# Which early load carries the first k, and which k the weights' loads wait for, in a fused linear-attention and GELU-MLP kernel

## The chip, the cores and the metric

The kernel runs on one core of a Trainium2 chip. The metric is the device time of one execution in microseconds (us). Before the change three runs gave 172.68, 172.98 and 173.50 us, so a median of 172.98. The profile was taken in an execution of its own, which took 173.12 us; its trace spans 171.3 us, and 1.8 us lie around the span.

## What is computed

A recurrent attention with a decay per key feature runs over 768 tokens in each of 4 batches and 8 heads of 48 features; its output, 3072 tokens of 384 features, goes through an MLP of width 2048 with the tanh form of GELU.

```
def _attn_ref(q, k, v, alpha):
    for t in range(S):
        state = alpha[:, :, t, :, None] * state + np.einsum('bhd,bhe->bhde', k[:, :, t], v[:, :, t])
        y[:, :, t] = np.einsum('bhd,bhde->bhe', q[:, :, t], state)

x = attn_out.transpose(0, 2, 1, 3).reshape(B * S, H * D)
h = x @ w_in
g = 0.5 * h * (1.0 + np.tanh(c * (h + 0.044715 * h * h * h)))
out = g @ w_out
```

## The kernel before

**Tiling.** The 768 tokens are cut into 6 chunks of 128. A *unit* is one chunk of two batches; there are 12 units, 0 to 11, and unit 0 and unit 1 are the two halves of chunk 0. In each unit the recurrence is done as matrix products: the logarithm of alpha (`ln`, on ScalarE, called ACT) is summed along the tokens by a product with a triangle of ones (`cum`, on TensorE, called PE), `b` and `binv` are its exponentials with either sign (ACT), `qp` and `kp` are q and k scaled by them (VectorE, called DVE), `t` turns them on PE and `ev` copies the turned tile out (ACT or DVE), `attn` is the product of turned k and q (PE), `mask` keeps its triangle (DVE), `vb` casts v (ACT or DVE), `y` is the attention output (PE), `x` copies it out, `tx` turns it and `xe` copies that. `kv` and `st` carry the state to the next chunk; `bend`, `end` and, from unit 3 on, `rows` (four 32-wide transposes on DVE, L466) prepare the decay of the state. Then `l1` (L684) is the first MLP product in 8 pieces of 6 matmuls for a unit, `gelu` follows on ACT, `l2` (L703) is the second product in 4 pieces of 4 matmuls for each batch of the unit, and `ot` and `store` bring the result out. A name such as `l10.6` is piece 6 of `l1` for unit 0, `kp0.1` the second `kp` of unit 0. In units 0 and 1 the two batches go through `ln`, `cum`, `qp`, `kp`, `t` and `attn` one by one.

**Buffers that order the work.** PSUM is given out by a planner: `ff` has 4 banks (for `l1`, `l2`, the `cum` of units 0 and 1, idle products and some `attn`), `yk` has 2 (for `t`, `y`, `tx`, `kv`), `ca` holds one tile. A task that takes a bank waits until its former users are done.

**Order.** `Scheduler.order` (L64) lists every task. Up to about 45 us the order is the list `FIRST` (L189), written out by hand: `P:` is PE, `V:` DVE, `A:` ACT, `G:` GpSimd (called POOL), `S:` SyncE (called SP). `fill.n` stands for n idle products of 512 columns (L318), which keep PE busy. Behind the list the planner picks by rank; `SHIFT` (L236) changes ranks, and `AFTER` (L242) adds a dependency. `W` and `LANDED` hold the planner's costs and landing times; they move only the planned order, and nothing in the program waits for them.

**Early loads.** `RINGS` (L185) lists the loads that SP or ACT issue, `load.0` to `load.11`: both alphas of unit 0 (`load.0`, `load.1`), then q and k of its first batch (`load.2`, `load.3`), q and k of its second batch (`load.4`, `load.5`), and the same six of unit 1. `BY_ACT = (2, 3,)` (L187) gives `load.2` and `load.3` to ACT. `LOADS` (L182) lists what POOL issues: v of unit 0 (`load.12`), `w_in` in four parts (`load.13`, `15`, `16`, `17`), v of unit 1 (`load.14`, between the first and second part), `w_out` in four parts, and the inputs of the later units. An entry `gatek 0 1` is a copy of one element of k on POOL (L343), which waits until that load has landed; everything that POOL issues behind it waits with it. So `gatea 0 1` holds the load of v until the second alpha of unit 0 is there, and `gatek 0 1` holds `w_in` until the k of the second batch of unit 0 is there. The program calls the two batches of a unit 0 and 1, which is what the last digit means.

The loads are L334 (SP and ACT), L337 (POOL, rows) and L359 (POOL, `w_in`).

Of the kernel before, what the change touches and what calls it, by code (L numbers as in the profile page):

```python
# [16 lines left out]
    cum=530, cum_packed=1500, t8=450, t4=225, attn=340, kv=170, inter=165, intra=203, tx=168, l1_4=655, l1_2=340, l2=651,  # L17
    qk2=880, qk1=500, ev8=610, ev4=350, mask=610, st=1065, st0=545, end=110, attn2=600, vb=320, vb_act=480, ring=1300, ring_issue=670, out=2050, lead=600, receipt=1400, receipt_hw=1000, xc=475, xe=275, ot=540,
    ev8_act=920, ev4_act=520, xc_act=385, xe_act=400, ot_act=450,
    strip=1700, cast=1450, weight=2080, dma=2100, issue=1100, wissue=760, sp=420, store=2600, turn=1250, landed=2200, xbar_qk=1500, xbar_x=1400, turn_lead=50, stored=300, turn_receipt=200, rows=1400, ones=205, late_qk=1700, late_x=1700, late_x6=500, piece=330, late_k=1500, piece_issue=450, begin=620, cast_0=1300, share=1200, cast_1=1900, ln_packed=1040, cold=380, t64=640, fill=216, zero=1100,  # L20
)
COST = {
    ("ACT", "b"): (385, 135), ("ACT", "binv"): (385, 135), ("ACT", "ev"): (600, 40), ("ACT", "gelu"): (510, 110),
# [151 lines left out]
class _Kernel:  # L175
# [3 lines left out]

    SPLIT = (2,)  # L180
    EARLY = (0, 1)
    LOADS = ('gatea 0 1', 'v0', 'gatek 0 1', 'in 0', 'v1', 'in 1', 'in 2', 'in 3', 'out 0', 'out 1', '2a', 'out 2', '2b', 'out 3', '3', '4', '5', '6', 'a7', 'q7', 'hold k 5', 'k7', 'v7', 'a8', 'hold k 6', 'q8', 'k8', 'a9', 'hold k 7', 'v8', 'q9', 'k9', 'hold k 8', 'v9', 'a10', 'q10', 'hold x 7', 'k10', 'a11', 'hold k 9', 'q11', 'k11', 'v10', 'hold k 10', 'v11')  # L182

    PACKED, CUM_FF, R = (0, 1), (0, 1), 4
    RINGS = (('a', 0, 0, 1), ('a', 0, 1, 2), ('q', 0, 0, 1), ('k', 0, 0, 1), ('q', 0, 1, 2), ('k', 0, 1, 2),  # L185
             ('a', 1, 0, 1), ('a', 1, 1, 2), ('q', 1, 0, 1), ('k', 1, 0, 1), ('q', 1, 1, 2), ('k', 1, 1, 2))
    BY_ACT = (2, 3,)  # L187

    FIRST = """  # L189
        A:table.0 A:load.2 A:load.3 S:load.0 S:load.1 S:load.4 A:ln0.0 S:load.5 P:fill.7 P:cum0.0 A:ln0.1 G:gate.0 G:load.12 S:load.6 P:cum0.1 A:b0.0 S:load.7  # L190
        A:bend0.0 V:qp0.0 A:binv0.0 A:binv0.1 S:load.8 V:kp0.0 P:fill.2 P:t0.0 A:b0.1 V:ev0.0 P:fill.1 P:t0.1 S:load.9 A:ev0.1 V:qp0.1 S:load.10 A:bend0.1
        P:fill.3 P:attn0.0 V:kp0.1 G:gate.1 S:load.11 P:t0.2 G:load.13 V:mask0.0 A:ev0.2 P:t0.3 G:load.14 V:mask0.1 A:ev0.3 P:fill.1 P:t0.4 V:ev0.4 P:fill.1
        P:attn0.1 A:ln1.0 G:load.15 P:t0.5 V:mask0.3 P:cum1.0 A:ev0.5 G:load.16 V:vb0.0 A:ln1.1 V:end0.0 P:y0.0 V:mask0.2 G:load.17 P:kv0.0 A:binv1.0 P:cum1.1
        V:st0.0 A:x0.0 G:load.18 A:vb0.1 V:kp1.0 P:tx0.0 A:b1.0 P:y0.1 V:xe0.0 G:load.19 V:qp1.0 P:t1.1 A:x0.1 A:bend1.0 G:load.20 A:b1.1 P:fill.1 P:t1.0
        A:ev1.0 V:ev1.1 G:load.21 V:qp1.1 P:fill.1 P:kv0.1 V:st0.1 G:load.22 A:binv1.1 P:tx0.1 P:attn1.0 V:xe0.1 G:load.23 P:t1.2 V:kp1.1 P:l10.0 A:ev1.2
        G:load.24 V:mask1.0 P:t1.3 A:bend1.1 P:t1.4 V:mask1.1 G:load.25 A:ev1.3 P:l10.1 V:ev1.4 G:load.26 A:vb1.0 P:t1.5 P:attn1.1 G:load.27 V:ev1.5 P:y1.0
        G:load.28 P:l10.3 V:end1.0 V:vb1.1 V:mask1.2 G:load.29 A:gelu0.0 P:kv1.0 P:l10.2 V:mask1.3 A:x1.0 G:load.30 P:l10.5 A:gelu0.1 V:st1.0 A:gelu0.3 P:y1.1
        G:load.31 P:l10.4 A:gelu0.5 V:x1.1 P:tx1.0 A:gelu0.2 P:tx1.1 P:l10.6 G:load.32 V:xe1.1 A:gelu0.4 V:xe1.0 P:l10.7 A:gelu0.6 G:load.33 P:l11.0 A:gelu0.7
        P:l11.6 A:gelu1.0 P:l11.5 A:gelu1.6 P:l11.7 A:gelu1.5 P:l11.2 A:gelu1.7 P:l11.4 A:gelu1.2 P:l11.3 A:gelu1.4 P:l11.1 A:gelu1.3 P:kv1.1 P:l20.0
        A:gelu1.1 P:l20.4 P:l20.1 A:ln2.0 P:l20.2 P:cum2.0 P:l20.5 A:b2.0 A:binv2.0 P:l20.9 A:bend2.0 V:kp2.0 A:ln2.1 P:l20.6 V:st1.1 P:cum2.1 V:qp2.0 P:l20.8  # L200
        A:b2.1 A:binv2.1 P:t2.0 P:l20.3 V:kp2.1 A:ev2.0 V:qp2.1 P:l20.10 A:bend2.1 P:attn2.0 P:t2.1 V:mask2.1 P:l20.7 A:ev2.1 V:mask2.0 P:l20.14 A:ln3.0
        P:attn2.1 P:y2.0 V:mask2.2 P:l20.13 V:mask2.3 P:l20.12 V:x2.0 P:cum3.0 A:ot0.0 V:ot0.1 P:y2.1 A:ot0.2 S:store0.0 S:store0.1 P:tx2.0 P:l20.11 A:x2.1
        S:store0.2 V:xe2.0 A:b3.0 P:tx2.1 P:l20.15 V:xe2.1 A:binv3.0 V:end2.0 P:l12.0 V:ot0.3 P:l12.1 V:qp3.0 S:store0.3 P:kv2.0 P:l12.2 V:st2.0
        A:gelu2.0 P:l12.3 V:kp3.0 A:gelu2.1 P:l12.4 A:gelu2.2 P:t3.0 A:gelu2.3 V:ev3.0 A:gelu2.4 P:l12.5
    """.split()
    LANDED = {"load.0": 2800, "load.1": 3400, "load.2": 4400, "load.3": 5000, "load.4": 6000, "load.5": 7300, "load.12": 10100, "load.6": 9200, "load.7":
              10000, "load.8": 10500, "load.9": 11000, "load.10": 11600, "load.11": 12000, "load.13": 14100, "load.14": 16000, "load.15":
              17800, "load.16": 19200, "load.17": 21100, "load.18": 23500, "load.19": 24800, "load.20": 26400, "load.21": 27100, "load.22":
              27900, "load.23": 28300, "load.24": 30100, "load.25": 31000, "load.26": 31900, "load.27": 32600, "load.28": 32900, "load.29":
              34800, "load.30": 36700, "load.31": 38400, "load.32": 41200, "load.33": 42600}  # L210

    NARROW = (0, 1)

# [20 lines left out]
    PIECES = (0, 192, 320, 384)  # L234

    SHIFT = {  # L236
        'b10.0': 557, 'b6.0': 10, 'b9.0': -173, 'binv8.0': -756, 'kp9.0': -733, 'kv3.1': -567, 'mask3.1': 47, 'mask7.2': -293, 'mask7.3': -104,
        'mask8.0': 10, 'mask8.1': 43, 'qp6.0': -300, 'qp7.0': 100, 'rows7.0': 100, 'st3.0': 127, 'tx3.1': -30, 'tx4.0': -60, 'tx5.0': 1204,
        'x7.1': -400,
    }  # L240

    AFTER = {  # L242
        'cum6.0': 'y4.0',
    }

    ROW_ENDS = (3, 4, 5, 6, 7, 8, 9)
# [484 lines left out]
    def tasks(self):  # L731
        s = self.s = Scheduler(self.BUFS, self.fill, 40000, self.FIRST, self.LANDED)
        B, NCH = self.B, self.NCH
# [341 lines left out]
```

## Time and profile before

| what | value |
|---|---|
| median of three runs | 172.98 us |
| the profiled execution | 173.12 us |
| its span | 171.3 us |
| PE busy | 165.6 us (97%) |
| ACT busy | 128.8 us (75%) |
| DVE busy | 102.8 us (60%) |
| POOL busy | 58.8 us (34%) |
| DMA, mean | 175 GB/s |

Busy time is the time in which an engine executes. A PE that executes idle products counts as busy. The chain of waits is followed back from the last instruction: at each step it goes to what released the instruction, so it names the work on which the end hangs. The timeline shows the instructions of an engine in order, with the idle time in front of them and what ended it. "To landing" of a load is the time from its issue until its last part is in SBUF. All times below count from the start of the span.

### The profile page before, as it was taken

Reading aid. Unit: us, or ns where it says so; the run is one execution under the profiler, and the core shown is the slowest. Engines: PE = TensorE matmul, PEld = TensorE weight load, DVE = VectorE, ACT = ScalarE, POOL = GpSimd, SP = SyncE. Lnnn points to the kernel's source line nnn. Section 1 sums busy time; section 2 is a strip of 40 time slices with the busy share of each in tenths; the row PEclk is TensorE's granted clock in tenths of the full one; section 3 lists DMA queues with packets and bytes.
Section 4 is the critical chain, followed back from the end, with each engine's and each line's share of the span. In section 5 each row is a group of like instructions: output and inputs, shape, how many; then the busy total and the mean of one; then the engine's idle time right before and its main releaser. Section 6 shows DMA issues by size and latency. Waiting matters only on the chain.

```text
span 171.3 us, 4477 instructions
## 1 busy us (share of the span) xinstructions
PE 165.6 (97%) x1851; PEld 130.3 (76%) x1853; DVE 102.8 (60%) x210; ACT 128.8 (75%) x214; POOL 58.8 (34%) x71
## 2 busy tenths in 40 slices
PE   7889999999999999999999999999999999999993
PEld 2556999666886896796697697797796796886973
DVE  6399940166889999797896798695640825100000
ACT  3568899846979897788798599399798992572831
POOL 2397446997655400096008009402503000000000
PEclk9999999999999999999999999999999999999999
DMA  4999999999999999789998999996799961401102
GB/s 129 308 255 230 204 245 232 226 228 203 214 305 200 236 253 167 97 182 243 216 221 102 211 167 142 236 255 141 208 139 150 126 157 31 138 0 50 46 0 92
DMA packets 53652, 29.91 MB, mean 175 GB/s; under 512 B 41728, under 2 KB 50048, under 8 KB 53632
## 3 DMA queue, kind: packets, MB, share of 16 engines
q0 software_dynamic: 26464, 17.70, 63.0%
q1 hardware_dynamic: 26624, 11.54, 33.8%
q10 hardware_dynamic: 544, 0.39, 0.8%
q8 instruction: 14, 0.23, 0.6%
q14 instruction: 6, 0.05, 0.1%
HBM read 25.17 MB, written 4.72 MB: 174 GB/s over the span
## 4 chain that ended last, share of the span: by engine, by line
PE 91%; DMA 3%; ACT 3%; DVE 1%; issue 0%; DVEq 0%
PE hT L684 37%; PE acc L703 37%; PE at L583 4%; DMA k<-in_k_dram 3%; PE yps L649 2%; PE cum L416 2%; PE kv L600 2%; PE qkT_ps L488 2%; PE yps L563 1%; PE xT_ps L672 1%; PE yps L641 1%; ACT qkT L506 1%; PE k_ps L534 1%; ACT L309 1%; PE qkT_ps L519 1%; PE idle L318 1%
## 5 line engine op out<-in xcount | busy, mean ns | idle before, releaser
L703 PE MATMUL acc<-w_out,gT 128*128 128x384 bf16 (+3 forms) x416 | 68.5, 314 | 0.0
L684 PE MATMUL hT<-xT,w_in 128*128 128x256 bf16 x576 | 67.9, 273 | 0.0
L684 PEld LDWEIGHTS <-w_in 128*128 128x128 bf16 x576 | 61.5, 114 | 1.4
L690 ACT ACTIVATE gT<-hT 128x512 bf16<-128x512 f32 x96 | 54.1, 604 | 5.7 <-PE hT L684 2.6
L703 PEld LDWEIGHTS <-gT 128*128 128x128 bf16 x416 | 37.2, 98 | 20.2
L590 DVE TENSOR_TENSOR atm<-at,ut 128x512 bf16<-128x512 f32 x48 | 30.2, 683 | 6.6 <-PE at L583 6.4
L715 ACT COPY ot<-acc 128x384 f32<-128x384 f32 (+3 forms) x21 | 9.3, 446 | 17.0 <-PE acc L703 16.3
L478 DVE TENSOR_TENSOR kp<-k,binv 128x768 bf16<-128x768 f32 (+1 forms) x15 | 11.9, 795 | 15.6 <-ACT binv L450 14.9
L351 POOL CAST gate<-qkT 128x1 f32<-128x1 bf16 x6 | 1.1, 189 | 50.2 <-DMA qkT<-kp 50.2
L478 DVE TENSOR_TENSOR qp<-q,b 128x768 bf16<-128x768 f32 (+1 forms) x15 | 11.9, 792 | 8.1 <-ACT b L450 8.1
L450 ACT ACTIVATE b<-cum 128x768 f32<-128x768 f32 (+1 forms) x15 | 10.3, 684 | 5.3 <-PE cum L416 3.4
L337 POOL DMA_DIRECT2D k<-in_k_dram x11 | 12.2, 1110 | 5.6 <-DMA vb<-in_v_dram 2.5
L337 POOL DMA_DIRECT2D a<-in_alpha_dram x11 | 12.3, 1117 | 3.5 <-DMA w_in<-in_moe_w_in_dram 1.3
L337 POOL DMA_DIRECT2D vb<-in_v_dram x11 | 12.2, 1109 | 3.7 <-PE hT L684 0.9
L337 POOL DMA_DIRECT2D q<-in_q_dram x11 | 12.2, 1113 | 3.5 <-DMA w_out<-in_moe_w_out_dram 1.0
L466 DVE STREAM_TRANSPOSE rows<-b 32x256 f32<-32x256 f32 x28 | 12.3, 439 | 0.5
L309 ACT ACT_TABLE_LOAD x9 | 11.5, 1283 | 0.9 <-PEq L1059 0.7
L450 ACT ACTIVATE binv<-cum 128x768 bf16<-128x768 f32 (+1 forms) x15 | 10.2, 683 | 2.2 <-PE cum L416 2.1
L690 ACT ACT_TABLE_LOAD x9 | 11.5, 1283 | 0.2
L623 DVE TENSOR_TENSOR stmp<-kv,st 128x384 f32<-128x384 f32 x16 | 8.8, 553 | 1.2 <-PE kv L600 1.1
L626 DVE TENSOR_TENSOR st<-stmp,ends 128x384 bf16<-128x384 f32 x16 | 8.9, 558 | 0.6
L399 ACT ACTIVATE la<-a 128x768 f16<-128x768 f32 (+1 forms) x11 | 8.7, 787 | 0.1
(83 smaller groups left out, 142.7 us busy)
## 6 DMA issues: line engine op xcount, KB each, us to landing
out_dram<-ot SPq DMA_DIRECT2D x19, 192.0 KB, 4.6
a<-in_alpha_dram POOLq DMA_DIRECT2D x9, 384.0 KB, 9.6
q<-in_q_dram POOLq DMA_DIRECT2D x9, 384.0 KB, 8.6
k<-in_k_dram POOLq DMA_DIRECT2D x9, 384.0 KB, 9.2
vb<-in_v_dram POOLq DMA_DIRECT2D x9, 192.0 KB, 9.5
w_in<-in_moe_w_in_dram POOLq DMA_DIRECT2D x4, 384.0 KB, 8.9
w_out<-in_moe_w_out_dram POOLq DMA_DIRECT2D x4, 384.0 KB, 11.1
out_dram<-ot SPq DMA_DIRECT2D x9, 96.0 KB, 5.0
```

Of the source, the lines that this page charges most:

```text
L309: nc.scalar.add_instruction(mybir.InstLoadActFuncSet(name=nc.get_next_instruction_name(), act_func_set_id=i, engine=mybir.EngineType.Activ ...
L337: dma(u[t][:, lo:hi].rearrange("t b h d -> t (b h) d"), src.rearrange("b h s d -> s (b h) d")[c * C:(c + 1) * C])
L450: self.nc.scalar.activation(u[n].rearrange("t i h d -> t i (h d)")[:, lo:hi], cum, AF.Exp, scale=1.0 if n == "b" else -1.0)
L466: nc.vector.transpose(t[f:f + 32], bass.AP(last.tensor, last.offset + o * D + 32 * half, [list(last.ap[0]), [2 * D, H], [1, 32]]))
L478: self.nc.vector.tensor_tensor(out, rows, b, op=ALU.mult)
L590: self.nc.vector.tensor_tensor(u["atm", i][:, o], u["at", i][o], self.ut[:, None, :].to_broadcast([self.C, self.H // 2, self.C]), op=ALU.mult)
L623: nc.vector.tensor_tensor(s, acc, old, op=ALU.add)
L626: nc.vector.tensor_tensor(new.rearrange("f p (o d) -> f (p o) d", o=2), acc.rearrange("f p (o d) -> f (p o) d", o=2), ends, op=ALU.mult)
L684: self.nc.tensor.matmul(h[:, s], w_in[:, j, nt % 4 + s], self.xT[c % self.NX][:, lo:hi, j], start=j == 0, stop=j == self.NKT - 1, skip_gro ...
L690: return lambda e: self.nc.scalar.activation(self.gT[c % self.NG][:, nt:nt + 2, lo * self.C:hi * self.C], f.pop(("h", c, lo, nt)), AF.Gelu ...
L703: self.nc.tensor.matmul(f["acc", c, b][:, lo:hi], self.gT[c % self.NG][:, nt, b * self.C:(b + 1) * self.C], self.w_out[:, nt, lo:hi], star ...
L715: self.copy(e)(f["ot", c, b][:, sl], f["acc", c, b] if half is None else f["acc", c, b, half][:, sl])
```

## The change

Three things are edited, and the order is made anew around them.

1. `BY_ACT` loses `load.3`: the k of the first batch of unit 0 is issued by SP, third in its queue, behind both alphas. ACT issues only `load.2`.
2. `gatek 0 1` becomes `gatek 0 0`: POOL's loads of the weights wait for that first k.
3. `FIRST`, `LANDED`, `W["rows"]`, `SHIFT` and `AFTER` are new. The same products stand in another order.

The core of the diff, with the whole list of early steps up to the first pieces of `l1`:

```diff
-    LOADS = ('gatea 0 1', 'v0', 'gatek 0 1', 'in 0', 'v1', 'in 1', 'in 2', 'in 3', 'out 0', 'out 1', '2a', 'out 2', '2b', 'out 3', '3', '4', '5', '6', 'a7', 'q7', 'hold k 5', 'k7', 'v7', 'a8', 'hold k 6', 'q8', 'k8', 'a9', 'hold k 7', 'v8', 'q9', 'k9', 'hold k 8', 'v9', 'a10', 'q10', 'hold x 7', 'k10', 'a11', 'hold k 9', 'q11', 'k11', 'v10', 'hold k 10', 'v11')
+    LOADS = ('gatea 0 1', 'v0', 'gatek 0 0', 'in 0', 'v1', 'in 1', 'in 2', 'in 3', 'out 0', 'out 1', '2a', 'out 2', '2b', 'out 3', '3', '4', '5', '6', 'a7', 'q7', 'hold k 5', 'k7', 'v7', 'a8', 'hold k 6', 'q8', 'k8', 'a9', 'hold k 7', 'v8', 'q9', 'k9', 'hold k 8', 'v9', 'a10', 'q10', 'hold x 7', 'k10', 'a11', 'hold k 9', 'q11', 'k11', 'v10', 'hold k 10', 'v11')
...
-    BY_ACT = (2, 3,)
+    BY_ACT = (2,)
...
-        A:table.0 A:load.2 A:load.3 S:load.0 S:load.1 S:load.4 A:ln0.0 S:load.5 P:fill.7 P:cum0.0 A:ln0.1 G:gate.0 G:load.12 S:load.6 P:cum0.1 A:b0.0 S:load.7
-        A:bend0.0 V:qp0.0 A:binv0.0 A:binv0.1 S:load.8 V:kp0.0 P:fill.2 P:t0.0 A:b0.1 V:ev0.0 P:fill.1 P:t0.1 S:load.9 A:ev0.1 V:qp0.1 S:load.10 A:bend0.1
-        P:fill.3 P:attn0.0 V:kp0.1 G:gate.1 S:load.11 P:t0.2 G:load.13 V:mask0.0 A:ev0.2 P:t0.3 G:load.14 V:mask0.1 A:ev0.3 P:fill.1 P:t0.4 V:ev0.4 P:fill.1
-        P:attn0.1 A:ln1.0 G:load.15 P:t0.5 V:mask0.3 P:cum1.0 A:ev0.5 G:load.16 V:vb0.0 A:ln1.1 V:end0.0 P:y0.0 V:mask0.2 G:load.17 P:kv0.0 A:binv1.0 P:cum1.1
-        V:st0.0 A:x0.0 G:load.18 A:vb0.1 V:kp1.0 P:tx0.0 A:b1.0 P:y0.1 V:xe0.0 G:load.19 V:qp1.0 P:t1.1 A:x0.1 A:bend1.0 G:load.20 A:b1.1 P:fill.1 P:t1.0
-        A:ev1.0 V:ev1.1 G:load.21 V:qp1.1 P:fill.1 P:kv0.1 V:st0.1 G:load.22 A:binv1.1 P:tx0.1 P:attn1.0 V:xe0.1 G:load.23 P:t1.2 V:kp1.1 P:l10.0 A:ev1.2
-        G:load.24 V:mask1.0 P:t1.3 A:bend1.1 P:t1.4 V:mask1.1 G:load.25 A:ev1.3 P:l10.1 V:ev1.4 G:load.26 A:vb1.0 P:t1.5 P:attn1.1 G:load.27 V:ev1.5 P:y1.0
-        G:load.28 P:l10.3 V:end1.0 V:vb1.1 V:mask1.2 G:load.29 A:gelu0.0 P:kv1.0 P:l10.2 V:mask1.3 A:x1.0 G:load.30 P:l10.5 A:gelu0.1 V:st1.0 A:gelu0.3 P:y1.1
-        G:load.31 P:l10.4 A:gelu0.5 V:x1.1 P:tx1.0 A:gelu0.2 P:tx1.1 P:l10.6 G:load.32 V:xe1.1 A:gelu0.4 V:xe1.0 P:l10.7 A:gelu0.6 G:load.33 P:l11.0 A:gelu0.7
...
+        S:load.0 A:table.0 A:load.2 S:load.1 A:ln0.0 S:load.3 A:ln0.1 S:load.4 S:load.5 P:fill.7 G:gate.0 G:load.12 S:load.6 S:load.7 S:load.8 P:fill.2
+        P:cum0.0 P:fill.1 A:b0.0 A:bend0.0 P:cum0.1 A:binv0.0 V:qp0.0 A:b0.1 P:t0.0 V:kp0.0 S:load.9 S:load.10 A:bend0.1 A:binv0.1 V:end0.0 P:fill.3 G:gate.1
+        S:load.11 G:load.13 A:ev0.0 P:t0.1 A:ev0.1 V:qp0.1 G:load.14 A:ln1.0 P:fill.1 V:kp0.1 P:fill.1 G:load.15 P:t0.2 P:attn0.0 V:ev0.2 P:t0.3 G:load.16
+        A:ev0.3 P:cum1.0 V:mask0.0 V:mask0.1 P:attn0.1 V:mask0.3 G:load.17 V:mask0.2 A:ln1.1 P:t0.4 A:b1.0 G:load.18 G:load.19 P:cum1.1 P:t0.5 A:binv1.0
+        G:load.20 A:bend1.0 A:ev0.4 A:ev0.5 V:vb0.0 P:fill.1 G:load.21 V:vb0.1 P:y0.0 V:kp1.0 A:x0.0 P:kv0.0 A:b1.1 V:st0.0 P:y0.1 A:x0.1 V:qp1.0 P:tx0.0
+        V:xe0.0 P:t1.1 A:ev1.1 P:t1.0 V:qp1.1 P:fill.1 G:load.22 V:ev1.0 A:bend1.1 A:binv1.1 P:tx0.1 V:end1.0 P:t1.2 V:xe0.1 P:attn1.0 P:l10.0 V:kp1.1
+        V:mask1.0 A:ev1.2 P:t1.3 V:mask1.1 A:ev1.3 P:kv0.1 P:l10.1 V:st0.1 A:vb1.0 G:load.23 V:vb1.1 A:gelu0.0 P:t1.5 V:ev1.5 P:attn1.1 G:load.24 P:t1.4
+        G:load.25 V:ev1.4 P:l10.2 P:y1.0 P:l10.3 P:kv1.0 P:l10.5 A:x1.0 V:mask1.2 G:load.26 V:mask1.3 V:st1.0 A:gelu0.1 P:y1.1 V:x1.1 P:l10.4 P:tx1.0 P:tx1.1
+        A:gelu0.3 A:gelu0.2 P:l10.7 A:gelu0.5 V:xe1.1 P:l10.6 V:xe1.0 G:load.27 A:gelu0.4 A:gelu0.7 P:l11.0 P:l11.2 A:gelu0.6 P:l11.3 A:gelu1.0 G:load.28
...
     SHIFT = {
-        'b10.0': 557, 'b6.0': 10, 'b9.0': -173, 'binv8.0': -756, 'kp9.0': -733, 'kv3.1': -567, 'mask3.1': 47, 'mask7.2': -293, 'mask7.3': -104,
-        'mask8.0': 10, 'mask8.1': 43, 'qp6.0': -300, 'qp7.0': 100, 'rows7.0': 100, 'st3.0': 127, 'tx3.1': -30, 'tx4.0': -60, 'tx5.0': 1204,
-        'x7.1': -400,
+        'b8.0': 40, 'binv10.0': -10, 'binv9.0': -100, 'cum6.0': 801, 'end4.0': 510, 'kp7.0': 17, 'kv4.0': 441, 'kv5.0': -993, 'ln5.0': -303,
+        'qp6.0': 200, 'rows7.0': -664, 'st4.0': 343, 't4.0': -490828, 'tx3.0': -946, 'tx4.0': 328,
     }

     AFTER = {
-        'cum6.0': 'y4.0',
+        'cum6.0': 'l23.4', 'kv3.0': 'l13.0', 'kv3.1': 'cum5.0', 'kv6.1': 'l25.3', 'kv7.0': 'l26.3', 'y3.0': 'l22.4',
     }
```

In the new order PE, from the start: 7 and 2 idle products, `cum0.0`, 1 idle, `cum0.1`, `t0.0`, 3 idle, `t0.1`, 2 idle, `t0.2`, `attn0.0`. DVE around unit 7's `rows`: `x5.0 st5.0 rows7.0 st5.1 ot4.1 qp7.0`; before it was `x5.0 st5.0 st5.1 kp7.0 qp7.0`, the four masks of unit 6, and then `rows7.0`, while `ot4.1` stood on ACT.

## Prediction

> **What bounds the kernel now.** First the page: where does PE stop?
>
> ```profile
> span 171.3 us, 4477 instructions
> PE 165.6 (97%) x1851; PEld 130.3 (76%) x1853; DVE 102.8 (60%) x210; ACT 128.8 (75%) x214; POOL 58.8 (34%) x71
> PE   7889999999999999999999999999999999999993
> ```
>
> PE is short of work in the first three slices of 4.3 us, thinly in the fourth, and in the last. From about 17 us the products follow without a hole and their number doesn't change: behind 23 us the change can only lose. Next the chain of waits, its head and the place where the last piece of w_in is first used:
>
> ```profile
> 1.92 5.66 DMA k<-in_k_dram
> ...
> 7.67 0.57 DVE kp L478
> ...
> 22.99 0.34 PE xT_ps L672 x6
> 23.32 6.55 PE hT L684 x60
> ```
>
> It begins with the load that is moved: k lands at 7.58 and frees kp. A chain names what came last at each step, though, not what is second. So I read the timelines of POOL and DVE, then the landings of the tiles v and w_in:
>
> ```profile
> 5.65 1.29 POOL L337 DMA_DIRECT2D v<-in_v_dram  x1
> 8.45 0.18 POOL L343 COPY gate<-k 128x1 f32<-128x1 f32 x1 [1.51 <-DMA k<-in_k_dram]
> 8.91 0.74 POOL L359 DMA_DIRECT2D w_in<-in_moe_w_in_dram  x1 [0.29 <-issue]
> ...
> 10.83 2.25 POOL L359 DMA_DIRECT2D w_in<-in_moe_w_in_dram  x3
> ```
>
> ```profile
> 12.44 0.36 DVE L427 CAST vb<-v 128x384 bf16<-128x384 f32 x1
> ```
>
> ```profile
> DMA to landing us min/median/max: 6.4/8.9/10.7
> ```
>
> The v of unit 0 is issued at 5.65 and takes 6.8 us (the lowest landing of tile v): 12.4, just when DVE casts it. And the last part of w_in, third of the three issues of 0.75 us from 10.83, starts at 12.33 and takes the longest, 10.7 us: 23.0. PE first needs it for `l10.6`, which starts at 23.16 in PE's timeline. Two more landings thus stand 0 and 0.15 us behind the chain, and neither is the k that moves.
>
> Is there room for these to land sooner? The table of stretches (last two columns: DMA share and GB/s):
>
> ```profile
> 8.00:12.00 4.00, 3.23 (x41) 2.04 (x43) 3.75 (x8) 2.16 (x5) 3.27 (x5) 1.00 1.09 280
> 12.00:16.00 4.00, 3.59 (x57) 2.82 (x56) 3.99 (x10) 3.80 (x10) 3.53 (x6) 1.00 1.17 244
> 16.00:20.00 4.00, 3.94 (x61) 3.35 (x61) 3.77 (x10) 3.06 (x7) 1.91 (x3) 1.00 1.20 193
> ```
>
> The 16 DMA engines are full (a share of 1 and above) from 8 us on; from 4 to 8 it is 0.99. Issue plus time to landing, from the DMA view of one issue at a time, gives 12.4 for v, 12.9 and 13.4 for the last q and k of unit 1, 15.3 for the first w_in, 17.6 for the second v, 19.2, 21.1 and 23.0 for the rest of w_in. Each lands one transfer's time behind the one before. A load issued earlier only stands longer in that line.
>
> **The change part by part.**
>
> *The k on SP.* It is issued third, at 2.19 instead of 1.92. The trace doesn't show it there. Earliest: behind the second alpha (5.48) by one step of SP's line (0.6, between landings of unit 1): 6.1. Latest: 7.58 as now. I take 6.8. The other loads of SP slip by one issue (0.66), and the two that wait for a landing (q and k of unit 1, issued at 7.80 and 8.44) go at about 6.9 and 7.5.
>
> *The head of the list.* Nine idle products stand before `cum0.0`, not seven. Seven take 3.17 from 1.19, so they start 0.427 apart: `cum0.0` starts at 5.03, not 4.48. But PE is quicker by then: the first cum takes 1.39 from start to end, the second 0.89. It ends at 5.92 instead of 5.87: 0.05. (Were it still slow, 0.5 later, the wait for v and then that for w_in, below, would cover it.) Then b ends at 6.46, qp starts at 6.49, kp at 6.97 (qp's pitch 0.47; binv is done at 6.91), not 7.67. Yet `t0.0` (7.10, 0.22) and three idle products (0.65) are ahead of `t0.1`: it starts at 7.97, not 8.29. So k has until 7.3 at no cost, and its 0.7 us are worth 0.32. `attn0.0` starts at 9.04, not 9.36.
>
> *The cover.* DVE then does ev (9.06 to 9.66) and four masks of 0.61: free at 12.10. The next is the cast of v, which lands at 12.4. So `vb0.0` starts at 12.44, as now, and `y0.0` at 12.85, against 12.86. The whole gain of k ends in the wait for v.
>
> *From y0.0 to l1.* Now 12.86 to 17.19, 4.33 us. In the new order the second cum of unit 1 (0.76) is ahead of the wait, `kv0.1` (0.17) behind `l10.0`. What is left goes by the two yk banks: y and x (0.92) give `y0.1` at 13.77, again 0.93 to `t1.1` at 14.70; t, ev on ACT (0.58) and waits 1.07 to `tx0.1` at 15.77; `t1.2` 16.10, `attn1.0` 16.32, `l10.0` 16.65. That is 3.80: a gain of 0.54.
>
> *From there to the last part of w_in.* Six pieces of l1 (0.655 each), three t, an attn, two y, two kv, two tx: 3.93+0.67+0.33+0.42+0.33+0.33 = 6.0, and 0.3 waiting for the third w_in at 21.1 (`l10.5`): 22.97. Then `l10.7` waits for 23.0 and starts at 23.03, against 23.16. Of 0.54 there stay **0.13**. Behind it both orders have the same ten pieces.
>
> *The gate.* POOL gets from the copy of k to the next issue in 0.46. It is free of v's issue at 6.94, so w_in is issued at about 7.4 instead of 8.91. Queued behind the gate are all later loads; none waits longer. I count nothing for 1.5 us of earlier issue, since the line of DMA hides it. Bounds: 0, and the whole 0.54 if w_in lands 0.5 sooner.
>
> *The later order.* The products are the same. I followed each PE task's inputs and banks by these durations and found one new wait. In stage 5 `rows7.0` (four transposes, 1.83) now stands between `st5.0` and `st5.1`, and `attn6.0` needs a bank that `st5.1` and `ot4.1`, both behind it on DVE, give back. From the start of `y5.0`: kv5.0 is done at 1.76, st 1.07, rows 1.83, st 1.07, ot 0.55, 0.05 to PE: 6.33. PE's work between: y 0.40, five l2 3.25, cum 0.33, two kv and two tx 0.66, two l1 1.31, and 0.10 that stands ahead of every attn: 6.05. So 0.28. The same way of counting gives waits of up to 0.2 in the order of before where the trace has none, so it is between 0 and 0.3; I take 0.15. The order of turns and stores on SP changes too; I found nobody who waits longer.
>
> Sum: −0.13 + 0.15 = 0.0 on the profiled execution's 173.12 (171.3 of span and 1.8 around it, untouched). The median of the runs is 0.14 lower, 172.98: **173.0 us, no change**. A measurement of this kernel can tell about 0.5% (0.86 us) from no change.
>
> **The rivals.**
>
> *The weights do land earlier.* For it: in stretches of 1 us the rate falls from 370 GB/s (8 to 9) to 254 and 224 (9 to 11), before the loads issued at 7.80 and 8.91 are there; the new order fills that, and 0.15 MB at 300 GB/s are 0.5 us. Against: the share stays at 0.99 and 1.04, so the engines are held by v rather than idle. If w_in lands 0.5 sooner and v with it, `l10.7` goes at 22.5: 172.4 to 172.5.
>
> *The loads of SP push v back (slower).* q and k of unit 1 are issued 0.9 us earlier, close to v's arrival. Mechanism: the DMA engines serve SP's and POOL's queues in turn, so v shares with them and lands last of the three, at up to 13.4 instead of 12.4. Then `l10.7` can go at 22.7+1.0 = 23.8: +0.6, and with the wait of stage 5 +0.9: 173.6 to 173.9. It decides from v at 12.9 on; below that w_in covers it. Against it: those three lie in line together from about 10 us (q and k 1.5 us behind their issue, which is what the first load needs before bytes move), and v, the double size, still lands first, then q and k 0.5 apart; taking turns would have let q pass v.
> [...]
>
> *The change does what it says and it pays in full*, because v comes sooner as well: its gate, the second alpha (5.48), no longer shares with a k on ACT's queue. With v at 12.1 DVE is the bound and the gain is 0.5 to 0.7, but only if w_in follows; so it is the first rival with its end at 172.3.
>
> **How the numbers follow.** No change as worked out (within 0.3): 0.55. Weights and v earlier: 0.20, of which 0.08 beyond 0.86 us, by something the walk misses. Slower by v: 0.17, of which 0.10 beyond. Something in the later order: 0.08, all beyond. So faster by over 0.5% 0.1, slower 0.2 (0.18 rounded), within 0.7. The range takes in both rivals, 172.3 to 173.9; what is left out is the 0.2 of larger surprises.
>
> **What would show it.** Right: kp's first start near 7.0, `vb` at 12.4 or later, the wait before the first l1 piece of the fourth w_in (PE idle just before 23.0), w_in's longest landing grown from 10.7 to about 12.2 because it is issued 1.5 earlier. Wrong: w_in landing at 22.5 or less; v at 13; a hole of PE before `attn6.0` over 0.3, or any other behind 24 us.

## The result: 2.6% slower, and the profile after

The changed kernel took 178.05 us (median of four executions, 176.38 to 178.50) against 172.94 beside it: a ratio of **1.026, 95% interval 1.023 to 1.030**. The prediction was no change, 173.0, in a range up to 173.9. The profiled execution took 177.86, with a span of 176.1: 4.8 more than before. Executions of one kernel scatter here, so a ratio counts only those within 1.5% of the fastest of that kernel, and the profile of a longer one is read for where transfers land, not for its time.

Where does PE stop now? First the page of the changed kernel (PE's line, PE's slices of 4.4 us, and the clock granted to it):

```profile
span 176.1 us, 4469 instructions
PE 167.2 (95%) x1852; PEld 131.3 (75%) x1853; DVE 99.9 (57%) x204; ACT 131.5 (75%) x220; POOL 59.3 (34%) x71
PE   7996999999999999999999999999499999999993
PEclk9999999999999999999999999999789999999999
```

Two slices are new: the fourth (13 to 18 us) and the 29th (123 to 128 us), and only from the second of them on is the clock low. The chain of waits has a step for each, and both are transfers that were not in it before:

```profile
0.73 0.74 SPq L333
7.47 10.38 DMA k<-in_k_dram
...
24.24 6.55 PE hT L683 x60
...
113.69 12.18 DMA qkT<-qp
126.41 0.85 PE at L582 x16
127.27 4.14 PE hT L683 x30
```

The step at 7.47 is the last load of SP, k of the second batch of unit 1 (`load.11`), 10.38 us to landing; in the kernel before that load was issued at 8.44 and took 5.0. The step at 113.69 is the DMA that turns qp of unit 9 (`turn9.0`), 12.18 us; before it took 3.0. (All line numbers are one lower than before.)

Put beside the old trace instruction by instruction, PE is 0.91 us late at `l11.0` (25.38 against 24.47) and 0.77 at the last l2 piece ahead of the hole; then 2.70 are lost before `attn9.0`, and 1.28 more until `l18.4`, while the clock is low. That makes 4.75 of the 4.8, and nothing changes behind it. So there are two losses: one **early**, one **late**.

**The early one.** POOL's timeline, and DVE's (its columns: start, duration, instruction, and in brackets the idle time before it and what ended it):

```profile
5.26 1.29 POOL L336 DMA_DIRECT2D v<-in_v_dram  x1
6.78 0.18 POOL L342 COPY gate<-k 128x1 f32<-128x1 f32 x1 [0.23 <-DMA k<-in_k_dram]
7.24 0.74 POOL L358 DMA_DIRECT2D w_in<-in_moe_w_in_dram  x1 [0.28 <-issue]
```

```profile
7.39 0.55 DVE L477 TENSOR_TENSOR kp<-k,binv 128x384 bf16<-128x384 f32 x1
...
12.52 0.62 DVE L426 CAST vb<-v 128x384 bf16<-128x384 f32 x2
...
15.65 0.56 DVE L477 TENSOR_TENSOR qp<-q,b 128x384 bf16<-128x384 f32 x1 [0.69 <-DMA q<-in_q_dram]
...
17.94 0.56 DVE L477 TENSOR_TENSOR kp<-k,binv 128x384 bf16<-128x384 f32 x1 [0.78 <-ACT qkT L505]
```

The first w_in goes 1.67 us earlier, as said. But w_in's tile view gives a longest landing of 12.2 us instead of 10.7: the weights are in at 22.85 instead of 23.00. What they overtook are the loads of SP. Landings in order, before and after:

| load | queue | before | after |
|---|---|---|---|
| v of unit 0 | POOL | 12.41 | 12.27 |
| k of unit 1, first batch | SP | 10.78 | 12.70 |
| w_in, first part | POOL | 15.32 | 15.16 |
| q of unit 1, second batch | SP | 12.93 | 15.56 |
| v of unit 1 | POOL | 17.65 | 17.49 |
| k of unit 1, second batch | SP | 13.44 | 17.85 |

After, the two queues land one for one. `qp1.1` waits for its q until 15.65, and `kp1.1` starts at 17.94, 0.09 behind the landing of its k, where before it started at 17.06 with the k long there:

```profile
17.06 0.55 DVE L478 TENSOR_TENSOR kp<-k,binv 128x384 bf16<-128x384 f32 x1
```

(After, the bracket names a copy on ACT; what came last is the landing, as the row of k in the table and the same pair of times in five more kernels below show.) Below, q1.1 and k1.1 are q and k of the second batch of unit 1, k1.0 is the k of its first batch.

**The late one.** SP's timeline (issue time and how long the issue took), and PE's:

```profile
111.16 1.27 SPq L545 DMA_TRANSPOSE qkT<-kp  x1
112.52 1.07 SPq L727 DMA_DIRECT2D out_dram<-ot  x2
113.69 5.26 SPq L545 DMA_TRANSPOSE qkT<-qp  x1
```

```profile
125.91 0.50 PE L562 MATMUL yps<-st,qkT 64*128 64x48 bf16 x16 [2.63 <-DMA qkT<-qp]
```

`turn9.1` (kp of unit 9) is issued at 111.16, 1.05 us behind POOL's `load.60` (k of unit 10) and 0.10 ahead of `load.61` (alpha of unit 11). It takes 13.7 us to landing, `load.61` 13.2. Before, it was issued at 114.79, behind `turn8.2` (x of unit 8), 8.1 us after `load.60`, and took 3.4; `attn9.0` then started at 122.44 with no idle time before it:

```profile
114.79 1.23 SPq L546 DMA_TRANSPOSE qkT<-kp  x1
116.11 1.26 SPq L546 DMA_TRANSPOSE qkT<-qp  x1
```

```profile
122.44 0.37 PE L563 MATMUL yps<-st,qkT 64*128 64x48 bf16 x16
```

What the engines moved meanwhile is in the table of stretches (last three columns: clock, DMA share, GB/s), of the changed kernel and then of the kernel before:

```profile
116.00:120.00 4.00, 4.00 (x36) 3.04 (x35) 2.40 (x6) 3.59 (x7) 0.00 (x0) 1.00 1.27 101
120.00:124.00 4.00, 3.28 (x21) 1.76 (x18) 1.79 (x2) 3.05 (x6) 0.00 (x0) 1.00 1.28 107
124.00:128.00 4.00, 2.09 (x36) 1.69 (x37) 1.17 (x3) 1.14 (x1) 2.58 (x4) 0.67 0.93 211
```

```profile
116.00:120.00 4.00, 4.00 (x29) 2.76 (x28) 1.82 (x4) 3.97 (x7) 1.24 (x2) 1.00 0.69 148
120.00:124.00 4.00, 4.00 (x56) 2.74 (x55) 2.56 (x4) 3.09 (x5) 2.40 (x3) 1.00 0.79 209
```

In the changed kernel the share says full, but the rate is 101 and 107 GB/s, a third of the 306 that the same engines moved from 112 to 114 us. Before, they moved more at a lower share. That is what the experiments had to explain.

### The profile page after: what moved, and what is told of

The parts are those of the page before. It is cut to its first block, busy times and chain, and to the rows that moved or that the text cites. A ratio compares the mean times of both kernels' runs of the same rounds, so it can differ in the third digit from the quotient of the medians.

```text
span 176.1 us, 4469 instructions
## 1 busy us (share of the span) xinstructions
PE 167.2 (95%) x1852; PEld 131.3 (75%) x1853; DVE 99.9 (57%) x204; ACT 131.5 (75%) x220; POOL 59.3 (34%) x71
## 4 chain that ended last, share of the span: by engine, by line
PE 81%; DMA 13%; SPq 4%; issue 0%; DVE 0%; ACT 0%; DVEq 0%
PE hT L683 35%; PE acc L702 33%; DMA qkT<-qp 7%; DMA k<-in_k_dram 6%; SPq L333 4%; PE at L582 3%; PE cum L415 2%; PE kv L599 2%; PE yps L648 2%; PE yps L562 1%; PE xT_ps L671 1%; PE qkT_ps L487 1%; PE yps L640 1%; PE qkT_ps L518 1%; PE yps L637 0%
## 5 line engine op out<-in xcount | busy, mean ns | idle before, releaser
L683 PE MATMUL hT<-xT,w_in 128*128 128x256 bf16 x576 | 69.2, 275 | 0.0
L714 ACT COPY ot<-acc 128x384 f32<-128x384 f32 (+3 forms) x24 | 10.8, 452 | 15.8 <-PE acc L702 12.8
L336 POOL DMA_DIRECT2D q<-in_q_dram x11 | 12.2, 1109 | 5.5 <-issue 2.0
L336 POOL DMA_DIRECT2D k<-in_k_dram x11 | 12.2, 1107 | 5.2 <-DMA vb<-in_v_dram 2.3
L336 POOL DMA_DIRECT2D vb<-in_v_dram x11 | 12.2, 1106 | 3.5 <-issue 0.9
L505 ACT COPY qkT<-qkT_ps 128x512 bf16<-128x512 bf16 (+1 forms) x8 | 5.6, 695 | 4.3 <-PE qkT_ps L487 4.3
```

Source lines behind the costliest of these rows:

```text
L336: dma(u[t][:, lo:hi].rearrange("t b h d -> t (b h) d"), src.rearrange("b h s d -> s (b h) d")[c * C:(c + 1) * C])
L683: self.nc.tensor.matmul(h[:, s], w_in[:, j, nt % 4 + s], self.xT[c % self.NX][:, lo:hi, j], start=j == 0, stop=j == self.NKT - 1, skip_gro ...
L714: self.copy(e)(f["ot", c, b][:, sl], f["acc", c, b] if half is None else f["acc", c, b, half][:, sl])
```

## The experiments

The theory at the start (A) had two separate causes: the early gate lets the weights into the turns of SP's loads; the later order puts turns among POOL's loads. The rival (B) had one: the early 0.8 us alone shifts the later transfers into each other.

All executions of each kernel. The kernel before ran beside them 104 times: 172.35 to 175.22. Since kernels with the changed order scatter by up to 9 us, the table gives the spread of all executions beside the ratio.

| kernel | n | lowest | median | highest | over 176 | ratio (95%) |
|---|---|---|---|---|---|---|
| changed kernel | 4 | 176.38 | 178.05 | 178.50 | 4 | 1.026 (1.023 to 1.030) |
| a_again (the same once more) | 6 | 174.94 | 179.40 | 182.02 | 5 | – |
| a_gate_second | 10 | 173.00 | 174.65 | 181.30 | 3 | 1.002 (0.997 to 1.007) |
| a_old_late | 4 | 177.08 | 177.28 | 177.78 | 4 | 1.024 (1.018 to 1.030) |
| b_new_late | 4 | 177.18 | 180.16 | 184.48 | 4 | 1.030 (1.017 to 1.043) |
| b_gate_first | 10 | 172.47 | 172.74 | 173.49 | 0 | 0.997 (0.994 to 1.000) |
| b_gate_first_again | 12 | 172.62 | 173.15 | 173.78 | 0 | 1.001 (1.000 to 1.003) |
| b_k_on_sp | 12 | 172.72 | 173.54 | 174.15 | 0 | 1.002 (1.000 to 1.003) |
| b_k_sp_gate_first | 12 | 172.66 | 173.84 | 175.01 | 0 | 1.004 (1.001 to 1.006) |
| b_kp7_late | 12 | 172.99 | 173.30 | 174.61 | 0 | 1.001 (1.000 to 1.003) |
| a_tail_before | 6 | 174.11 | 175.56 | 176.63 | 1 | 1.012 (1.007 to 1.016) |
| a_gate_tail_before | 6 | 173.85 | 174.53 | 175.06 | 0 | 1.007 (1.004 to 1.009) |
| a_k_act_tail_before | 9 | 173.65 | 174.64 | 177.91 | 1 | 1.008 (1.005 to 1.012) |
| a_kp7_first | 6 | 174.64 | 175.26 | 177.25 | 2 | 1.015 (1.010 to 1.019) |
| a_a11_behind | 8 | 173.36 | 174.85 | 180.81 | 3 | 1.005 (1.001 to 1.009) |
| a_turn91_later | 9 | 173.76 | 176.29 | 182.41 | 5 | 1.010 (1.005 to 1.014) |
| a_gate_turn91 | 8 | 173.90 | 174.93 | 180.53 | 3 | 1.009 (1.006 to 1.012) |
| a_loads_held | 12 | 173.15 | 175.10 | 182.21 | 3 | 1.007 (1.004 to 1.010) |
| a_gate_loads_held | 6 | 173.52 | 173.96 | 180.53 | 2 | 1.003 (1.000 to 1.005) |

### One part undone, one part alone

a_gate_second, the changed kernel with `'gatek 0 1'` again:

> The changed kernel with the weights' loads held for k of the second batch again, all else as changed. Theory A (two separate causes): the loads of unit 1 get their turn back, q1.1 lands near 13 and k1.1 near 13.5 instead of 15.56 and 17.85, the last first-product piece of unit 0 starts near 23.2 instead of 24.07, and some 0.8 comes back; the hole ahead of the attn of unit 9 stays, because the turns of unit 7 still stand in the new order: about 177.2. Theory B (the late hole only comes from the early shift): with the early loss gone the hole goes too, about 173.0.

a_old_late, the changed kernel with the old `SHIFT`, `AFTER` and `rows=1400`:

> The changed kernel with the ranks and the added dependencies of before, so with the later order of before behind the new early part. Theory A: turn7.1 goes ahead of turn7.0 again, POOL's loads of units 8 to 10 start some 4 us earlier, no hole ahead of the attn of unit 9, granted clock 1.0 there; the early loss stays: 173.7 to 173.9. Theory B: the hole stays, 177 to 178.

b_new_late, the kernel before with the new ones:

> The kernel before with the changed ranks and added dependencies alone; gate, k's queue and the early list as before. Theory A: turn7.0 ahead of turn7.1, POOL's loads 54 to 61 some 3 to 4 us later, the turns of unit 9 among loads 60 and 61, a hole of 2 to 3 us and a lower clock behind it: about 177. Theory B: no early shift, so no collision: 173.0.

b_gate_first, the kernel before with one entry changed:

```diff
-    LOADS = ('gatea 0 1', 'v0', 'gatek 0 1', ...
+    LOADS = ('gatea 0 1', 'v0', 'gatek 0 0', ...
```

> The kernel before with the one entry changed that holds the weights' loads: they wait for k of the first batch (still on ACT, landed at 7.58), all else as before. The first weights' load is then issued near 8.0 instead of 8.9, between q1.1 (7.80) and k1.1 (8.44) on SP. Theory A: the DMA engines serve SP's and POOL's queues in turn, so k1.1, perhaps q1.1 too, lands behind the first weights (15 to 18 instead of 13.4): 173.3 to 173.9. If the loads are served in the order in which they arrive, q1.1 stays at 13 and the time at 173.0. Theory B: a small shift is enough for the late hole: over 176.

**Early.** a_gate_second has q1.1 at 12.74, k1.1 at 13.99, `kp1.1` at 16.72 and the last kv of unit 1 at 29.80 instead of 30.62: the 0.82 came back, as A had it. In b_gate_first the gate alone cost nothing, against A: the first w_in was issued at 7.39, q1.1 at 6.97, ahead of it, and q1.1 landed at 12.99; k1.1 landed at 16.70 and `kp1.1` started 0.09 behind it, still no later than in the kernel before (17.06). In the changed kernel q1.1 was issued ahead of the first w_in as well (6.81 against 7.24) and landed behind it, at 15.56. What differs is the line of loads ahead of it on SP: with k on ACT, k1.0 was in at 10.17, in the changed kernel at 12.70.

**Late.** Here both theories missed. a_gate_second runs from 173.0 to 181.3, neither 177.2 nor 173.0: five of its ten executions are at 173.0 to 173.7, level with the kernel before, and three are over 176. The new later order is bad without any early shift (b_new_late, all four above 177, `turn9.1` 13.3 us to landing). And a_old_late, though its time is the one B had, is no test: behind another early list the planner makes another order from the same ranks; in its trace PE waited 2.7 us for masks on DVE and there was no hole at unit 9. So from here on the order behind the early list is written out task by task, and nothing is planned anew.

### The later order of before behind the new early list

```diff
+    def replay(self, order):
+        rest = [x.split(":") for x in self.REST]
+        names, named = {n for _, n in rest}, self.s.named
+        order = [t for t in order if t.name not in names]
...
-        order = self.s.order()
+        order = self.replay(self.s.order())
```

`REST` lists the tasks with their engines. a_tail_before is the changed kernel with the `REST` of before; a_gate_tail_before has `'gatek 0 1'` as well; a_k_act_tail_before has `BY_ACT = (2, 3,)` and the early gate.

> The changed kernel up to the end of the early list (k on SP, weights held for k of the first batch, the new list), and behind it every instruction in exactly the order and on the engine of before: nothing is planned anew. Theory A (late loss from the order of units 6 to 9): kp6.0 stands ahead of rows6.0 again, turn6.1 is issued near 72.5 to 73 ahead of load 48 and lands in under 3 us, the gate behind it opens near 77.3 instead of 82.06, no hole ahead of the attn of unit 9; only the early loss is left: 173.6 to 174.0. Theory B (the early shift of 0.8 us alone tips the later loads over): over 176.

> As the run with the later order of before, and the weights' loads held for k of the second batch again; k stays on SP and the early list stays new. Theory A: k1.0 still lands behind v of unit 0 (near 12.2), but q1.1 and k1.1 land near 12.7 and 14.0, ahead of the first weights, and 0.8 comes back: 172.8 to 173.2. If the early loss comes from the new early list or from k on SP by itself: 173.6 to 174.0.

> As the run with the later order of before, with the weights held for k of the first batch, but that k back on ACT. SP's loads of unit 1 are each one place further ahead: k1.0 lands near 10.2, q1.1 near 13, ahead of the first weights, only k1.1 behind them near 16.7. Theory A (it takes both edits to push q1.1 behind the weights): 172.7 to 173.2. If the gate alone makes the loss: 173.6 to 174.0.

The mix has a seam of its own, which I hadn't seen: `ev3.0` and `ev3.1` both fall to ACT, and `attn3.0` waits 0.59 us for the second. So 173.3 became 174.5 where the early loss was nil (a_gate_tail_before: 0.59 of it is this wait and 0.33 one for a turn of unit 8). All three took longer than was expected of them. But no profile of the three has a hole at unit 9; in a_tail_before `turn9.1` took 3.2 us though everything was 2.8 us late. That is against B: a shift alone doesn't do it. On the new list the early gate costs something even with k on ACT: in a_k_act_tail_before k1.1 landed at 17.42 and the last kv of unit 1 started at 30.20, against 15.91 and 29.75 in a_gate_tail_before.

### The two early edits on the kernel before, one by one

b_k_on_sp has `BY_ACT = (2,)` and `S:load.3` behind `S:load.1`; b_k_sp_gate_first has the early gate too. Everything else is the kernel before.

> The kernel before with one early edit: k of the first batch goes by SP's queue, third, behind both alphas; the weights still wait for k of the second batch; every other instruction in its place. Theory A (it takes k on SP and the early gate together): q1.1 and k1.1 still arrive ahead of the first weights and land by 14, nothing lost: 172.6 to 173.3. If k on SP loses by itself, since each later load of SP stands one place further back: 173.6 or more, with k1.0 or q1.0 behind v of unit 0 and l11.0 later than 24.5.

> The kernel before with both early edits (k on SP, weights held for that k) but with its own early list and its own later order; every other instruction in its place. Theory A: q1.1 lands behind the first weights (15.5 or later) and k1.1 behind the second big load (17.8 or later), and kp1.1 and the kv of unit 1 are 0.9 to 2 us later than before: 173.8 to 175.2, and runs that scatter more than those of the kernel before. If the new early list makes the loss: 172.6 to 173.2, as with the gate alone.

> The kernel before with the one gate entry changed, as in the earlier run, whose interval reached from 0.994 to 1.000: measured again, to tell a small gain from none. Weights in some 0.1 to 0.8 us earlier, q1.1 ahead of them, k1.1 near 16.7, just in time for its kp: 172.4 to 173.1. If k1.1 slips by one more load in many executions, the gain is gone: 173.1 to 173.6.

b_k_on_sp fell between its two expectations, and its profile shows another price: v of unit 0 landed at 12.80 instead of 12.41, DVE waited 1.18 us for it, `kp1.1` started at 17.55 (k1.1 was in at 15.50) and the last kv of unit 1 at 30.20 instead of 29.71. So k on SP can push v back, as the prediction's slower rival had it. b_k_sp_gate_first: v at 12.10, q1.1 at 14.86, k1.1 at 17.41, `kp1.1` at 17.51 instead of 17.06: 0.4% slower, just at the lower end of what was expected, and the delay of `kp1.1` is 0.45, half of the least expected. The gate alone, measured again, gains nothing: the 0.997 of the first time didn't come again. In the new list the price of the early gate is plain. From six profiles of that list with the gate early (the start of `kp1.1`, then of `kv1.1`, the last kv of unit 1):

| kernel | k1.1 landed | kp1.1 | kv1.1 | difference |
|---|---|---|---|---|
| a_k_act_tail_before | 17.42 | 17.52 | 30.20 | 12.68 |
| a_kp7_first | 17.73 | 17.82 | 30.50 | 12.68 |
| changed kernel | 17.85 | 17.94 | 30.62 | 12.68 |
| a_old_late | 18.24 | 18.33 | 31.02 | 12.69 |
| a_turn91_later | 18.31 | 18.41 | 31.09 | 12.68 |
| a_tail_before | 19.09 | 19.19 | 31.87 | 12.68 |

`kp1.1` starts 0.09 to 0.10 behind the landing, and PE follows it to the hundredth. a_loads_held fits as well (17.12, 17.22, 29.90). Two do not: in a_again `kp1.1` (17.33) was no longer held by k (16.82), and in a_a11_behind the granted clock was 0.61, 0.50, 0.50 and 0.68 in the stretches of 2 us from 14 to 22 us (`kv1.1` at 32.92). The early loss is the landing of one load, and it varies with the execution: in eight profiles with the early code of the changed kernel `kp1.1` starts anywhere from 17.22 to 19.19. In the four profiles of the new list with the old gate it starts at 16.42 to 16.87, ahead of all eight, and three of them have `kv1.1` at 29.75 to 29.80; the fourth is told below.

### Which step of the later order?

In unit 7 the new order puts `kp7.0` nine instructions later on DVE (90.42 against 83.99), and with it `turn7.1`, which opens the gate of POOL's loads 54 to 56. a_kp7_first moves it back in the changed kernel, b_kp7_late does the reverse in the kernel before:

```diff
-DVE: st5.0 rows7.0 st5.1 ot4.1 qp7.0 mask6.0 mask6.1 mask6.2 mask6.3 end7.0 kp7.0
+DVE: st5.0 rows7.0 kp7.0 st5.1 ot4.1 qp7.0 mask6.0 mask6.1 mask6.2 mask6.3 end7.0
-SP: store4.1 turn7.0 turn7.1
+SP: turn7.1 store4.1 turn7.0
```

> The changed kernel with two instructions moved and all else in its place: kp7.0 on DVE directly behind rows7.0 (it stood nine instructions later), and its turn7.1 on SP ahead of store4.1 and turn7.0. Theory A (the later loss comes from the turn of k of unit 7, which opens the gate of POOL's loads 54 to 56): turn7.1 issued near 86.5, that gate opens near 90.5 to 92 instead of 94.33, loads 57 to 61 start 2 us earlier or more, the hole ahead of the attn of unit 9 shrinks under 1 us: 173.6 to 175.2, the early loss left. If the hole comes from turn9.1 standing ahead of turn8.2, or from the gate of unit 6 alone: 177 to 178.

> The kernel before with the opposite of that edit, all else in its place: kp7.0 on DVE behind the four masks of unit 6 and rows7.0, turn7.1 on SP behind store4.1 and turn7.0. Theory A: turn7.1 issued near 91, the gate of loads 54 to 56 opens near 94 instead of 89.66, turn8.1 falls among those loads and takes 6 us or more instead of 3.6, loads 57 to 61 start some 3 us later, and the turns of unit 9 end late: 174.5 to 177. If a late k turn alone does nothing (the other moves of the later order are needed): 172.8 to 173.4.

a_kp7_first took 175.26, and the hole went (`attn9.0` starts with no idle time before it): `turn9.1` 7.8 us, clock 1.00. It has a price of its own, 0.65 us in which `attn6.0` waits for the `ot` that now stands behind `kp7.0` on DVE. With the early 0.79 (30.50 against 29.71) that is 1.44, and the profiled execution took 174.64, 1.5 more than that of the kernel before. But the reason given was wrong. Its loads 57 to 61 were issued at 106.18 to 110.88, against 106.39 to 111.26 with the hole; the gate had opened earlier and `turn8.1` lost that again. And a late `kp7.0` on the kernel before cost nothing (1.001). What differs at the place between a_kp7_first and the changed kernel is the turn itself: `turn9.1` is issued 2.2 us behind `load.60`, not 1.05.

### The turn among the loads

So theory C: a turn whose packets share the DMA engines with POOL's big loads slows both, far beyond the sum of their bytes. a_a11_behind puts `load.61` behind the gate that waits for `turn9.1` (its expectation still has the narrower form of the theory, one load), a_loads_held puts both there; a_turn91_later moves the turn instead:

```diff
-POOL: gate.6 load.60 load.61 gate.7 load.62
+POOL: gate.6 load.60 gate.7 load.61 load.62     (a_a11_behind)
+POOL: gate.6 gate.7 load.60 load.61 load.62     (a_loads_held)
-SP: store6.1 turn9.1 store6.2 store6.3 turn9.0
+SP: store6.1 store6.2 store6.3 turn9.1 turn9.0  (a_turn91_later)
```

> The changed kernel with every instruction in its place, but one: POOL issues load 61 (alpha of unit 11) behind the gate that waits for turn9.1, not ahead of it. Theory A (turn9.1 and turn9.0 are slow since load 61 flies beside them): turn9.1 lands near 118 instead of 124.84, the hole ahead of the attn of unit 9 goes, the clock stays at 1.0: 173.6 to 174.3. If the turns are slow because of loads 57 to 60 or of the stores between them, turn9.1 lands at 121 or later and the time stays over 176.

> The changed kernel with one instruction moved on SP: turn9.1 behind store6.2 and store6.3, not ahead of them; all else in its place. So it is issued about 1.3 us later, near 112.5. Theory C (turns whose small packets share the DMA engines with POOL's loads 60 and 61 slow both down, far more than the sum of their bytes; the later the turn, the less they overlap): turn9.1 lands earlier although it is issued later, near 120 instead of 124.84, turn9.0 near 121.5, the hole ahead of the attn of unit 9 is under 1 us and the clock stays at 1.0: 174.0 to 175.6. Theory A in its first form (only an earlier gate for loads 54 to 61 helps): no gain, or a loss by the delay, 177.5 to 179.

> The changed kernel with one entry moved on POOL: the gate that waits for turn9.1 stands ahead of loads 60 and 61 (k of unit 10, alpha of unit 11), not behind them; all else in its place. Theory C: turn9.1 shares the engines only with loads 57 to 59, which are in by 115, and lands near 117 to 118; loads 60 and 61 follow from there and land near 123 and 125; k of unit 10 is then up to 1.5 us late for its kp; no crawl, no low clock: 174.3 to 176. If the turns crawl for another reason (their own order, the stores beside them), turn9.1 still lands near 124 and the time stays at 177 or over.

> The changed kernel with two things undone: the weights wait for k of the second batch again, and turn9.1 stands behind store6.2 and store6.3. If the early loss is the gate's and the late loss is the overlap of turn9.1 with loads 60 and 61, nothing of the loss is left: 172.9 to 173.6, with k on SP and the rest of the new order still there. If the new order has another price, 174 or more.

> The changed kernel once more, with the same instructions in the same order on every engine, for more executions than the first four and a second profile. Theory C (the late loss is an overlap of turns with POOL's loads, which one execution meets and another does not): times spread from about 174 to over 178, the profile again with turn9.1 beside load 60 and 12 us or more to landing where it is slow. If the loss is fixed by the order: 176.4 to 178.5 again.

> The changed kernel with two things undone: the weights wait for k of the second batch again, and POOL's loads 60 and 61 stand behind the gate that waits for turn9.1. Theory C: kv1.1 near 29.8, turn9.1 near 116, l18.0 near 123.2: the fastest executions at 172.6 to 173.2, the median 173.0 to 174.6, since other turns (units 6, 8 and 10) still meet loads. If the later order has a price of its own besides the overlap: no execution under 174.

a_loads_held is the clearest: the same instructions, the turn issued at 110.44 (111.16 in the changed kernel, 110.95 in a_again), two loads taken from beside it. Its profile is of the fastest of its 12 executions. SP's timeline, PE's at unit 9, and the stretches:

```profile
110.44 1.28 SPq L588 DMA_TRANSPOSE qkT<-kp  x1
111.81 1.01 SPq L770 DMA_DIRECT2D out_dram<-ot  x2
112.92 2.69 SPq L588 DMA_TRANSPOSE qkT<-qp  x1
```

```profile
122.50 0.37 PE L605 MATMUL yps<-st,qkT 64*128 64x48 bf16 x16
```

```profile
116.00:120.00 4.00, 4.00 (x35) 2.76 (x33) 2.14 (x4) 3.59 (x6) 3.02 (x4) 1.00 0.82 200
120.00:124.00 4.00, 4.00 (x55) 2.74 (x54) 1.99 (x3) 3.05 (x5) 2.90 (x3) 1.00 1.05 253
124.00:128.00 4.00, 4.00 (x51) 3.99 (x50) 2.80 (x5) 3.77 (x8) 0.00 (x0) 1.00 1.48 195
```

`turn9.1` lands after 6.0 us, `turn9.0` after 4.9, PE has no idle time before `attn9.0`, the clock is 1.00, and the span is 171.4: that of before, with both early edits and the rest of the new order still there. From 116 to 124 us the engines move 1.8 MB (4 us at 200 and 4 at 253 GB/s) where the changed kernel moved 0.8 at a higher share. a_again, the same order without that edit, has the slow turns again: 13.7 and 12.0 us, against 13.7 and 12.2. The other runs give the window (time from the issue of `load.60` to that of `turn9.1`, and the turn's time to landing):

| kernel | behind load.60 | to landing |
|---|---|---|
| a_a11_behind | 0.17 | 13.4 |
| a_turn91_later | 0.58 | 14.6 |
| changed kernel, a_again | 1.05, 1.04 | 13.7, 13.7 |
| a_gate_turn91 | 1.43 | 14.9 |
| b_new_late | 1.55 | 13.3 |
| a_kp7_first | 2.18 | 7.8 |
| before, a_tail_before | 8.1, 7.9 | 3.4, 3.2 |
| a_gate_second (turn ahead of load.60) | −1.54 | 7.4 |
| a_loads_held, a_gate_loads_held (ahead) | −6.7, −6.4 | 6.0, 5.6 |

Every `turn9.1` issued within 0.2 to 1.6 us behind `load.60` took 13 to 15 us; no other `turn9.1` did. That is a finding about these two transfers and no rule for any load: in a_kp7_first the turn was issued 1.04 us behind `load.61`, also 384 KB, and took 7.8. The window also says why a_a11_behind and a_turn91_later missed in their profiles: a_a11_behind left `load.60` beside the turn, and in a_turn91_later the loads had come 2.2 us later, so that the moved turn fell just behind `load.60` again. Other executions of both ran at 173.4 to 174.1. In a_gate_second the collision came later: `turn8.2` took 10.8 us among loads 62 to 64. And a_gate_turn91, expected at 172.9 to 173.6, took 174.93: its profile has the turn in the window as well, so it tells of the window and not of the sum.

With gate and loads undone together (a_gate_loads_held) the fastest execution, 173.52, is 0.3 above the range that was expected for it, and the ratio 1.003, from four of six executions: in these, nearly all of the loss is these two, and the rest of the new order costs little. Its `kv1.1` missed, though: 30.69 instead of the 29.8 expected. `kp1.1` was in time (16.87), but PE ran at a granted clock of 0.73, 0.50 and 0.92 in the stretches 14 to 16, 16 to 18 and 18 to 20 us. So an execution can also lose time in the first 20 us by the clock, with either gate.

What this doesn't settle: with the two loads held, 3 of 12 executions (2 of 6 with the gate undone too) still took over 176 us, up to 182. Other turns of the new order (units 6, 8 and 10) still meet loads, but no profile caught such an execution with the loads held, so where those lost their time stays open. It also stays open why packets of a turn and of a load disturb each other so much. No version beat the kernel before.

## Why the prediction was wrong, step by step

- **"A load issued earlier only stands longer in that line."** Right for the weights (22.85 against 23.00; longest landing 12.2, as said), wrong for the other queue. There was no one line: SP's and POOL's loads landed in turn (POOL 12.27, SP 12.70, POOL 15.16, SP 15.56, POOL 17.49, SP 17.85). The step that failed is the gate, *"Queued behind the gate are all later loads; none waits longer"*, counted at nothing. It looked behind the gate; who waited longer was on SP. Price: 0.82 in PE by the trace (30.62 against 29.80 with the gate undone).
- **The slower rival had the mechanism that fits this trace and the wrong victim.** It let SP's loads push v back, to 13; v landed at 12.27 and k of unit 1 at 17.85. Its mechanism, queues served in turn, was an assumption, set aside because the landings of before fitted arrival order. (There the first w_in was issued at 8.91, behind SP's last load at 8.44.) Now q and k of unit 1, issued at 6.81 and 7.47, landed (15.56 and 17.85) behind a w_in and a v issued after them, at 7.24 and 7.97 (landed at 15.16 and 17.49): arrival order fails, and these landings agree with taking turns; from 12 to 14 us SP's queue moved 0.18 MB and POOL's 0.29, in the kernel before 0.04 and 0.45. How the engines choose among the packets of two queues no run shows. And b_k_on_sp shows the victim that the rival named, with v at 12.80.
- **k on SP, 6.8:** landed at 6.64. Right; `kp` started at 7.39, not 6.97, since the first cum was still slow (1.35, not 0.89), which the working had allowed for.
- **The cover by v:** the time was right, `vb` at 12.52 and `y0.0` at 12.93 (12.85 forecast), the reason by luck: v was in at 12.27, and DVE came to `vb` only then, since its four masks started at 10.10 and not at 9.66.
- **From `y0.0` to `l10.0` 3.80:** 4.58, by the wait for q1.1 (0.69 idle).
- **The wait of stage 5, 0.15:** about 0.1. Right.
- **"The order of turns and stores on SP changes too; I found nobody who waits longer."** This step cost the most, 2.70 and 1.28 of clock. The walk followed each PE task's inputs by durations measured in the old order; a turn's time to landing isn't a duration of its own, but depends on what flies beside it (3.2 to 14.9 us for the same `turn9.1`). The prediction's own sign of being wrong, a hole of PE behind 24 us, is what the trace showed. The trace of before had the warning: `turn10.1`, issued 3.6 us behind load 62, took 8.1 us, a turn alone 2.7.
- **The chances:** 0.08 for something in the later order and a range to 173.9 were too tight for an edit that reorders every transfer behind 45 us.

## What to carry to other kernels

A gate in front of a queue can protect the other queues too (opened early, it made `kv1.1` 0.82 us later here): before opening it earlier, list what is still in flight elsewhere and who needs it. A transfer's time to landing isn't a property of the transfer (3.2 to 14.9 us for one turn here): when an order is made anew, set each DMA's issue beside all loads in flight, above all small-packet transposes beside big loads (with 256-byte and 4224-byte packets together the engines moved 101 and 107 GB/s here from 116 to 124 us, in a_loads_held 200 and 253). And when an order is tried that brings transfers closer together, look at the spread over many executions, not at one: here the median lay up to 4.5 us above the lowest time.

## What the runs showed of the hardware that was not expected

- **Transposes and big loads together.** Between 117 and 124 us of the changed kernel the slowest tenth of the loads' 4224-byte packets took 1.54 us or more, of the turns' 256-byte packets 0.21 us; with loads and stores alone (112 to 114) the former was 0.32, with turns and stores alone (125 to 126) the latter 0.018. Beside each other both queues were slower. SP then also held its next issue: 5.26 us for `turn9.0`, 1.26 in the kernel before.
- **The clock after a hole of PE.** PE stood 2.63 us before `attn9.0`; from 126 to 128 us the granted clock was 0.50 and from 128 to 130 it was 0.80, and 1.28 us were lost until `l18.4`. The length of one hole alone doesn't decide it in these runs: in a_gate_loads_held the clock fell after 14 us though no idle time of PE was over 0.78 us (PE was busy for 0.83 of the 2 us from 12 to 14), while in b_k_on_sp PE stood 1.38 us before `y0.0` (13.35) and the clock stayed at 1.00.
